# An attention and two feed-forward layers in one program: the causal mask's triangle made on GpSimd, the padding queries put in front

## The chip, the cores and the metric

One core of one Trainium2 chip runs the whole program. The metric is device time in microseconds; the runs shown of the kernel before took 1008.39, 1011.96 and 1009.94 us, median 1009.94. Five engines work side by side: TensorE (PE, with its weight loads as PEld), VectorE (DVE), ScalarE (ACT), GpSimd (POOL) and SyncE (SP, which issues all DMAs here). Each runs its own instructions in the order in which the program was written.

## The reference

Causal attention for 4 batches of 8 heads (576 positions, 64 columns a head), then two feed-forward layers over the 2304 tokens:

```python
scores = scale * q @ k.T                        # per head, 576 x 576
bias = -(cum[:, None] - cum[None, :])           # cum = cumsum(max(s, 0))
scores = where(causal, -1e9, scores + minimum(bias, 0))
attn = exp(scores - scores.max(-1))             # then / (sum + 1e-9)
x = attn @ v                                    # heads side by side: 2304 x 512
h = x @ w_in;  x = (h * cos(h)) @ w_out         # 512 -> 2048 -> 512
h = x @ w_in2; out = (max(h, 0) + log1p(exp(-abs(h)))) @ w_out2
```

## The kernel before

The program is in two parts. The attention takes the heads one after another (`emit_attention(u, ...)`, u from 0 to 31; keys and queries come in pairs of heads). The feed-forward layers follow, each in blocks of 512 or 256 tokens, with every float32 factor split into two parts and three matmuls for each product.

A head goes through these steps:

- **Maxima.** A softmax needs the largest score of each query. Six matmuls (list `MT`, L441, issued in L496 to L500) take 128 queries as weights (`taq`, 66 rows: 64 columns of the head and two for cum) against the keys they may see (`tak`). The list holds (query block, first key, width, column of the result, place in the bank). DVE reads the PSUM bank, adds `mask` and reduces to one number a query (L504). The queries are padded from 576 to 640 with the padding behind, so query block i sees keys up to 128(i+1) - 1: widths 128, 256, 384, 512 and 320 + 256, in all 1856 columns a head.
- **Maxima to rows.** DVE joins the last block's two results (L510), a matmul with `eye` transposes them, ACT copies them out (L516), and a POOL select spreads them over rows 96 to 128 of `taq` (L518, 32 x 640 elements), where rows of -1 in `tak` subtract them in the next product.
- **Scores.** Seven stretches of keys by queries in five banks (list `STL`, L442), keys on the partitions: a product with the low parts (`tbk`, `tbq`), then for the five stretches that hold a diagonal block a matmul of `tri` through `ident` (128 columns, 64 for the last), which adds -1e30 above the diagonal, then the main product (`tak`, `taq`, 128 rows). ACT takes the exponential of each bank into one of four buffers `pf` (L558).
- **Values.** `pf` times the values with a column of ones, float32 (two passes a matmul), summed in banks 5 to 7 (L570, `final` closes a sum); ACT copies the sums out (L532) and SP sends them to memory.

Rows 64 to 96 of `tak` and `taq` hold the two cum rows and otherwise zeros. There are three sets ("slots") of these buffers in the memory that the later weights (`wlate`) take over after the attention; POOL fills their constant parts at the start (L353 to L372), and `mask`, `ident`, `tri` and `eye` with selects (a select, `affine_select`, keeps an element or writes a fill value, by an affine test on its place).

The order of the instructions is made by a planner (`Planner.plan`, L95): every operation has a due time and a list of what it reads and writes; the planner steps through a modelled time with a cost for each operation (an engine and nanoseconds, such as 1000.0 for L518's select) and writes for each engine, among what is ready, the one due first, on PE with a term for weight loads. While PE has nothing ready at the start it writes filler matmuls (L376, `warm`, 256 columns each, to bank 7). So a changed cost or a changed list moves instructions on every engine, though their due times stay; what happens on the chip then is that each engine follows its own list and waits where something is not there yet. A part of the first layer's weights is converted on DVE and ACT during the attention (L421 to L438).

Of the kernel before, what the change touches and what calls it, by code (L numbers as in the profile page):

```python
# [8 lines left out]
F32 = mybir.dt.float32  # L9
# [13 lines left out]
QS = (0, 256, 576)  # L23
EARLY, SLOT = 8, 4992
# [10 lines left out]
BIG = -3.0e38  # L35
ONE_LO = 1.0 - 2.0 ** -24
# [181 lines left out]
def act_t(n, psum=False):  # L218
    return n * 0.8333 + (52 if psum else 93)
# [6 lines left out]
def build(tc, qk, v, s, w1, w2, out):  # L226
# [8 lines left out]
    def T(name, shape, dt=F32):  # L235
        return sb.tile(shape, dt, name=name, tag=name)
# [32 lines left out]
    ident = T("ident", [128, 128], BF16)  # L269
    tri = T("tri", [128, 128], BF16)  # L270
# [7 lines left out]
    lnb = T("lnb", [128, 1])  # L278
    sraw, cum = heads[0][0:32], heads[2][0:32]
# [55 lines left out]
    V.memset(zero, 0.0)  # L335
    V.memset(mask, 0.0)
    V.memset(ident, 1.0)
    V.memset(tri, 0.0)
# [9 lines left out]
    for i in (2, 0, 1):  # L348
# [4 lines left out]
        fill(vt, tak.bitcast(F32)[64:96, :, 0:S], 0.0, ag)  # L353
# [3 lines left out]
        fill(vt + 2, taq.bitcast(F32)[0:96, :, S:], 0.0, [(("cq", i), 0)])  # L357
        fill(vt + 3, taq.bitcast(F32)[64:96, :, 0:S], 0.0, [(("augq", i, h), "z") for h in range(2)])
        P.op(vt + 4, [(POOL, 700.0, lambda taq=taq: G.memset(taq.bitcast(F32)[64:66, :, 0:S], 1.0))], r=[(("augq", i, h), "z") for h in range(2)], w=[(("augq", i, h), 0) for h in range(2)])
        if i == 2:  # L360
            P.op(vt + 8, [(POOL, 660.0, lambda: G.affine_select(out=mask, in_=mask, pattern=[[-1, 640]], compare_op=ALU.is_ge, fill=BIG, base=512, channel_multiplier=1))],
                 (), [("mask", 0)])
            P.op(vt + 9, [(POOL, 250.0, lambda: G.affine_select(out=ident, in_=ident, pattern=[[-1, 128]], compare_op=ALU.is_equal, fill=0.0, base=0, channel_multiplier=1))],
                 (), [("ident", 0)])
            P.op(vt + 10, [(POOL, 250.0, lambda: G.affine_select(out=tri, in_=tri, pattern=[[1, 128]], compare_op=ALU.is_ge, fill=-1.0e30, base=0, channel_multiplier=-1))],  # L365
                 (), [("tri", 0)])
# [74 lines left out]
    MT = [[(4, 0, 320, 4, 0), (0, 0, 128, 0, 320)], [(1, 0, 256, 1, 0), (4, 320, 256, 9, 256)], [(2, 0, 384, 2, 0)], [(3, 0, 512, 3, 0)]]  # L441
# [9 lines left out]
    def emit_attention(u, at, st):  # L451
# [9 lines left out]
        if sl == 0:  # L461
# [3 lines left out]
            if u == 0:  # L465
                t = at(-8)
                for x in range(2):
                    dma(t + x, raw[:, x], qk[0, :, x], w=[kr[x]])
                    P.op(t + 2 * x + 4, [(ACT, act_t(S), lambda x=x: A.activation(tak[0:64, x, 0:S], raw[0:64, x], AF.Copy))], r=[kr[x]], w=[kk[x]])
                    P.op(t + 2 * x + 5, [(ACT, act_t(S), lambda x=x: A.activation(taq[0:64, x, 0:S], raw[64:128, x], AF.Copy, scale=0.125))], r=[kr[x]], w=[kq[x]])  # L470
# [64 lines left out]
        for x, lst in enumerate(STL):  # L535
# [4 lines left out]
            for i, (j, qs, off, w) in enumerate(lst):  # L540
# [3 lines left out]
                if x != 1:  # L544
                    ml.append((o[:, 0:min(w, 128)], ident, tri[:, :min(w, 128)], False, False, True, 0))
# [244 lines left out]
```

## Time and profile before

| | us |
|---|---|
| runs shown, median | 1009.94 |
| profiled execution | 1008.23 |
| its span | 1006.4 |
| PE busy | 998.8 (99%) |
| DVE busy | 690.5 |
| ACT busy | 604.0 |
| POOL busy | 51.2 |

The span runs from the first to the last instruction of the profiled execution; 1.8 us lie around it. A busy time is the union of an engine's instructions; matmuls overlap in the records, so that a matmul's own duration is longer than the step from one start to the next. TensorE's granted clock is 1.00, the full 2.4 GHz, in every window asked for. The attention runs until about 211 us, the feed-forward layers from there to the end.

### The profile page before, as it was taken

How to read it: one execution, taken by the hardware profiler on the slowest of the kernel's cores; microseconds unless marked ns; L12 is line 12 of the kernel's file. 1: busy time of each engine (PE TensorE's matmuls, PEld its weight loads, DVE VectorE, ACT ScalarE, POOL GpSimd, SP SyncE). 2: the span in 40 equal slices, each digit the busy share in tenths (PEclk: the TensorE clock that was granted, in tenths of full speed). 3: DMA queues.
4: the chain of work that ended last, by engine and by line, in shares of the span. 5: the costliest groups of instructions: out<-in, count | busy, mean ns of one | idle time of the engine just before them, and what ended most of it. 6: DMA issues, size and time to landing. Idle time of an engine off the chain costs nothing.

```text
span 1006.4 us, 14198 instructions
## 1 busy us (share of the span) xinstructions
PE 998.8 (99%) x5180; PEld 842.3 (84%) x5180; DVE 690.5 (69%) x1284; ACT 604.0 (60%) x1062; POOL 51.2 (5%) x68
## 2 busy tenths in 40 slices
PE   9999999999999999999999999999999999999998
PEld 7888888878888889988888888888888998888886
DVE  8889888879964536445357989995565756555553
ACT  5777777777655445555456668665454655445444
POOL 8111112100000000000000000000000000000000
PEclk9999999999999999999999999999999999999999
DMA  6676666663422212002012335221130201001001
GB/s 209 212 209 188 194 189 185 190 211 113 155 84 91 90 51 101 26 22 64 1 65 99 135 130 189 88 80 49 35 115 1 84 1 42 1 1 42 1 1 42
DMA packets 40488, 95.29 MB, mean 95 GB/s; under 512 B 7074, under 2 KB 13730, under 8 KB 36322
## 3 DMA queue, kind: packets, MB, share of 16 engines
q1 hardware_dynamic: 40418, 94.39, 29.5%
q8 instruction: 40, 0.66, 0.3%
q14 instruction: 30, 0.25, 0.1%
HBM read 66.87 MB, written 18.64 MB: 85 GB/s over the span
## 4 chain that ended last, share of the span: by engine, by line
PE 93%; DVE 2%; DMA 2%; POOL 1%; issue 1%; ACT 0%; SPq 0%; DVEq 0%; POOLq 0%; ACTq 0%
PE bank L322 93%; PE bank L376 1%; DMA stage<-w 1%; DVE bc L504 1%; DMA adram<-num 0%; POOL wlate L330 0%; DMA raw<-rdram 0%; DMA raw<-adram 0%; DVE wlate L488 0%; DVE wlate L486 0%; DVE conv L429 0%; DMA rd<-adram 0%; DVE xl L308 0%; DVE raw L614 0%; POOL tri L365 0%
## 5 line engine op out<-in xcount | busy, mean ns | idle before, releaser
L322 PE MATMUL bank<-xh,wearly 128*128 128x512 f32 (+1 forms) x640 | 193.8, 369 | 1.2 <-DVE pf L658 1.2
L322 PE MATMUL bank<-xh,wlate 128*128 128x512 f32 (+1 forms) x640 | 193.7, 368 | 0.0
L322 PE MATMUL bank<-ghi,wlate 128*128 128x512 f32 (+1 forms) x640 | 193.5, 368 | 0.0
L322 PE MATMUL bank<-ghi,wearly 128*128 128x512 f32 (+1 forms) x640 | 193.5, 368 | 0.0
L299 ACT ACTIVATE ghi<-pf 128x512 fp32r<-128x512 f32 (+1 forms) x160 | 93.8, 587 | 141.9 <-DVE pf L670 92.0
L308 DVE TENSOR_TENSOR glo<-pf,ghi 128x512 fp32r<-128x512 f32 (+1 forms) x160 | 102.0, 637 | 77.4 <-ACT ghi L299 76.9
L322 PE MATMUL bank<-wlate 128*128 128x320 f32 (+9 forms) x576 | 150.5, 363 | 1.3 <-POOL xl L330 1.2
L322 PEld LDWEIGHTS bank<-xh,wearly 128*128 128x128 f32 x640 | 117.3, 189 | 21.7 <-DVE pf L658 1.6
L322 PEld LDWEIGHTS bank<-ghi,wlate 128*128 128x128 f32 x640 | 117.3, 189 | 20.0
L322 PEld LDWEIGHTS bank<-xh,wlate 128*128 128x128 f32 x640 | 117.3, 189 | 19.9
L322 PEld LDWEIGHTS bank<-ghi,wearly 128*128 128x128 f32 x640 | 117.3, 189 | 19.8
L322 PE MATMUL bank<-pf,vf 128*65 128x320 f32 (+4 forms) x448 | 127.9, 384 | 0.0
L322 PE MATMUL bank<-xl,wearly 128*128 128x512 f32 (+1 forms) x320 | 117.9, 369 | 0.0
L322 PE MATMUL bank<-glo,wlate 128*128 128x512 f32 (+1 forms) x320 | 117.9, 368 | 0.0
L322 PE MATMUL bank<-xl,wlate 128*128 128x512 f32 (+1 forms) x320 | 117.8, 368 | 0.0
L322 PE MATMUL bank<-glo,wearly 128*128 128x512 f32 (+1 forms) x320 | 117.8, 368 | 0.0
L322 PEld LDWEIGHTS bank<-wlate 128*128 128x128 f32 (+1 forms) x576 | 95.5, 191 | 17.7 <-POOL xl L330 1.4
L666 DVE SCALAR_TENSOR_TENSOR bc<-pf 128x512 f32<-128x512 f32 (+1 forms) x80 | 51.0, 637 | 81.7 <-ACT pf L664 81.7
L504 DVE CUSTOM_DVE_ANT_0 bc<-bank,mask 128x384 bf16<-128x384 f32 (+3 forms) x192 | 82.0, 468 | 15.7 <-PE bank L322 10.8
L558 ACT ACTIVATE pf<-bank 128x256 f32<-128x256 f32 (+2 forms) x160 | 66.7, 433 | 38.1 <-PE bank L322 33.3
L654 DVE SCALAR_TENSOR_TENSOR pf<-pf,pf 128x512 f32<-128x512 f32 (+1 forms) x80 | 50.7, 635 | 56.3 <-ACT pf L652 56.3
L663 ACT ACTIVATE pf<-bank 128x512 f32<-128x512 f32 (+1 forms) x80 | 44.3, 554 | 68.4 <-PE bank L322 65.7
(75 smaller groups left out, 1331.5 us busy)
## 6 DMA issues: line engine op xcount, KB each, us to landing
stage<-w SPq DMA_DIRECT2D x32, 1024.0 KB
raw<-qk SPq DMA_DIRECT2D x15, 576.0 KB
wlate<-wlate SPq DMA_DIRECT2D x30, 288.0 KB
vf<-v SPq DMA_DIRECT2D x32, 160.0 KB
adram<-num SPq DMA_DIRECT2D x32, 146.2 KB
xdram<-num SPq DMA_DIRECT2D x18, 256.0 KB
out<-num SPq DMA_DIRECT2D x18, 256.0 KB
raw<-adram SPq DMA_DIRECT2D x32, 128.0 KB
```

The source lines that it names most:

```text
L299: opts.append((ACT, act_t(n, psum), (lambda: A.activation(o, i, AF.Copy, scale=1.0 if scale is None else scale))))
L308: return [(DVE, dve_t(n), lambda: V.tensor_tensor(o, a, hi.bitcast(F32), op=ALU.subtract))]
L322: X.matmul(o, a, b, start=st, stop=sp, skip_group_check=skip)
L376: X.matmul(bank[7][:, 0:256], zero[:, 0:128], zero, start=True, stop=True)
L504: P.op(tx + 1, [(DVE, dve_t(w, True) + DX, lambda bk=bk, off=off, w=w, mo=mo, col=col, pr=pr, jk=junk[i if x < 2 else x - 2]: V.tensor_ten ...
L558: P.op(tx + 3, [(ACT, act_t(wt, True) + AX, lambda pt=pt, bk=bk, wt=wt: A.activation(pt[:, :wt], bank[bk][:, :wt], AF.Exp))], r=[(("bank", ...
L654: P.op(te + 2, [(DVE, dve_t(n), lambda a0=a0, a1=a1: V.scalar_tensor_tensor(a1, a1, MAGIC, a0, op0=ALU.subtract, op1=ALU.subtract))], r=[( ...
L663: P.op(te, [(ACT, act_t(n, True), lambda a0=a0, hp=hp: A.activation(a0, hp, AF.Abs))], r=hr, w=[(k0, (tg, "a"))])
L666: P.op(te + 2, [(DVE, dve_t(n), lambda a0=a0, a2=a2: V.scalar_tensor_tensor(a2, a0, 2.0, a0, op0=ALU.subtract, op1=ALU.mult, reverse0=True))],
```

## The change

Three things are changed together.

The triangle: `tri`, `ident` and their five matmuls a head go. In their place POOL writes zeros above the diagonal into the exponentials, in place in `pf`, one select for each of the five diagonal blocks (128 x 128, the last 128 x 64), after ACT's exponential and before the product with the values. So that no exponential overflows before it is cleared, rows 66 to 96 of `tak` and `taq` now hold steps of 20 positions: their product is -1.27e30 or below where a key lies in a later step than its query. Two POOL selects a slot write these steps, in place of a memset of zeros in `tak`, one in `taq` and one of ones in its two cum rows.

The padding: the 64 padding queries stand in front (`QP` = 64), so query block i sees keys up to 128 i + 63: widths 64, 192, 320, 448 and 320 + 256, in all 1600. `MT` is written anew for it, again six matmuls in four banks. All blocks now reduce 128 rows.

The order: new selects stand in the planner with 220 + 1.4 ns an element; the due times are unchanged, and the planner makes new lists for all engines.

```diff
 QS = (0, 256, 576)
+QP = 640 - S
...
+STEP, FAR = 20, -1.2676506002282294e30
...
-    ident = T("ident", [128, 128], BF16)
-    tri = T("tri", [128, 128], BF16)
...
+    cst = T("cst", [128, 2])
...
+    V.memset(cst[:, 0:1], 1.0)
+    V.memset(cst[:, 1:2], 0.0)
+    V.memset(cst[64:66, 1:2], 1.0)
     V.memset(mask, 0.0)
-    V.memset(ident, 1.0)
-    V.memset(tri, 0.0)
...
-        fill(vt, tak.bitcast(F32)[64:96, :, 0:S], 0.0, ag)
+        P.op(vt, [(POOL, 1400.0, lambda tak=tak: G.affine_select(out=tak[64:96, :, 0:S], in_=cst[64:96, 0:1].unsqueeze(2).broadcast_to((32, 2, S)), pattern=[[0, 2], [1, S]],
+                                                                 compare_op=ALU.is_ge, fill=0.0, base=STEP, channel_multiplier=-STEP))], (), ag)
         fill(vt + 1, tak.bitcast(F32)[:, :, S:], 0.0, ck)
         fill(vt + 1.5, tak.bitcast(F32)[96:128, :, 0:S], -1.0, [(("cm", i), 0)])
         fill(vt + 2, tbk.bitcast(F32)[:, :, S:], 0.0, [(("cb", i), 0)])
-        fill(vt + 2, taq.bitcast(F32)[0:96, :, S:], 0.0, [(("cq", i), 0)])
-        fill(vt + 3, taq.bitcast(F32)[64:96, :, 0:S], 0.0, [(("augq", i, h), "z") for h in range(2)])
-        P.op(vt + 4, [(POOL, 700.0, lambda taq=taq: G.memset(taq.bitcast(F32)[64:66, :, 0:S], 1.0))], r=[(("augq", i, h), "z") for h in range(2)], w=[(("augq", i, h), 0) for h in range(2)])
+        fill(vt + 2, taq.bitcast(F32)[0:96, :, 0:QP], 0.0, [(("cq", i), 0)])
+        P.op(vt + 3, [(POOL, 1400.0, lambda taq=taq: G.affine_select(out=taq[64:96, :, QP:], in_=cst[64:96, 1:2].unsqueeze(2).broadcast_to((32, 2, S)), pattern=[[0, 2], [1, S]],
+                                                                     compare_op=ALU.is_ge, fill=FAR, base=STEP, channel_multiplier=-STEP))], (), [(("augq", i, h), 0) for h in range(2)])
         if i == 2:
             P.op(vt + 8, [(POOL, 660.0, lambda: G.affine_select(out=mask, in_=mask, pattern=[[-1, 640]], compare_op=ALU.is_ge, fill=BIG, base=512, channel_multiplier=1))],
                  (), [("mask", 0)])
-            P.op(vt + 9, [(POOL, 250.0, lambda: G.affine_select(out=ident, in_=ident, pattern=[[-1, 128]], compare_op=ALU.is_equal, fill=0.0, base=0, channel_multiplier=1))],
-                 (), [("ident", 0)])
-            P.op(vt + 10, [(POOL, 250.0, lambda: G.affine_select(out=tri, in_=tri, pattern=[[1, 128]], compare_op=ALU.is_ge, fill=-1.0e30, base=0, channel_multiplier=-1))],
-                 (), [("tri", 0)])
             for x in range(3):
...
-    MT = [[(4, 0, 320, 4, 0), (0, 0, 128, 0, 320)], [(1, 0, 256, 1, 0), (4, 320, 256, 9, 256)], [(2, 0, 384, 2, 0)], [(3, 0, 512, 3, 0)]]
+    MT = [[(4, 0, 320, 4, 0), (1, 0, 192, 1, 320)], [(3, 0, 448, 3, 0), (0, 0, 64, 0, 448)], [(2, 0, 320, 2, 0)], [(4, 320, 256, 9, 0)]]
...
-                    P.op(t + 2 * x + 5, [(ACT, act_t(S), lambda x=x: A.activation(taq[0:64, x, 0:S], raw[64:128, x], AF.Copy, scale=0.125))], r=[kr[x]], w=[kq[x]])
+                    P.op(t + 2 * x + 5, [(ACT, act_t(S), lambda x=x: A.activation(taq[0:64, x, QP:], raw[64:128, x], AF.Copy, scale=0.125))], r=[kr[x]], w=[kq[x]])
...
-                dma(t + 17, taq.bitcast(F32)[0:64, :, 0:S], tbq.bitcast(F32)[64:128], r=[(ktbq, pt_)], w=kq + ([("go", 0)] if u == 2 else []))
+                dma(t + 17, taq.bitcast(F32)[0:64, :, QP:], tbq.bitcast(F32)[64:128], r=[(ktbq, pt_)], w=kq + ([("go", 0)] if u == 2 else []))
...
-                mo = 512 - 128 * qi + k0
-                pr = min(128, S - qi * 128)
+                mo = 512 + QP - 128 * qi + k0
+                pr = 128
...
-            rr = [(y, pt_) for y in (ktbk, ktbq, ktbkl, ktbql, (ktak, sl), (ktaq, sl), (kaugk, sl))] + [(kaugq, 0), (("c", rg), 0), (("cm", rg), 0), (("cb", rg), 0), ("ident", 0), ("tri", 0)]
+            rr = [(y, pt_) for y in (ktbk, ktbq, ktbkl, ktbql, (ktak, sl), (ktaq, sl), (kaugk, sl))] + [(kaugq, 0), (("c", rg), 0), (("cm", rg), 0), (("cb", rg), 0)]
                 o = bank[bk][:, off:off + w]
                 ml = [(o, tbk[:, sl, ks], tbq[:, sl, qs:qs + w], i == 0, False, True, w)]
-                if x != 1:
-                    ml.append((o[:, 0:min(w, 128)], ident, tri[:, :min(w, 128)], False, False, True, 0))
-                ml.append((o, tak[:, sl, ks], taq[:, sl, qs:qs + w], False, True, True, w))
+                ml.append((o, tak[:, sl, ks], taq[:, sl, QP + qs:QP + qs + w], False, True, True, w))
...
             pt = pf[pi]
             P.op(tx + 3, [(ACT, act_t(wt, True) + AX, lambda pt=pt, bk=bk, wt=wt: A.activation(pt[:, :wt], bank[bk][:, :wt], AF.Exp))],
                  r=[(("bank", bk), bt)], w=[(("pf", pi), bt)], table="exp")
+            done = bt
+            for i, (j, qs, off, w) in enumerate(lst):
+                if qs == 128 * j:
+                    dw = min(w, 128)
+                    P.op(tx + 4 + i, [(POOL, 220.0 + 1.4 * dw, lambda z=pt[:, off:off + dw], dw=dw: G.affine_select(
+                        out=z, in_=z, pattern=[[1, dw]], compare_op=ALU.is_ge, fill=0.0, base=0, channel_multiplier=-1))],
+                        r=[(("pf", pi), done)], w=[(("pf", pi), (bt, i))])
+                    done = (bt, i)
...
-                    P.op(at(st["av"] + x * SD) + y, mms(ml), r=[(("vo", u % 3), 0), (("vf", u % 3), tg), (("pf", pi), bt)] + old, w=[(key, (tg, "av", got[e]))])
+                    P.op(at(st["av"] + x * SD) + y, mms(ml), r=[(("vo", u % 3), 0), (("vf", u % 3), tg), (("pf", pi), done)] + old, w=[(key, (tg, "av", got[e]))])
```

PE in the middle of the attention, before: from behind a head's second product with 448 score columns and one of 320 to the first product of the 448 exponentials with the values (`pf0_94`). `bank5` to `bank7` take the value products.

```order
L322 LDWEIGHTS ident_103
L322 MATMUL bank3_68<-tri_104,ident_103 128x128
L322 MATMUL bank7_72<-pf3_97,vf_98 65x320
L322 MATMUL bank3_68<-wlate_80 128x320
L322 MATMUL bank4_69<-wlate_80 128x192
L322 LDWEIGHTS ident_103
L322 MATMUL bank4_69<-tri_104,ident_103 128x128
L322 MATMUL bank4_69<-wlate_80 128x192
L322 MATMUL bank4_69<-wlate_80 128x64
L322 LDWEIGHTS ident_103
L322 MATMUL bank4_69<-tri_104,ident_103 128x64
L322 MATMUL bank6_71<-pf0_94,vf_98 65x128
```

PE at the like place now, from the two products of 448 columns on (in `bank1`; the exponentials are in `pf1_95`):

```order
L323 MATMUL bank1_66<-wlate_80 128x448 x2
L323 MATMUL bank0_65<-wlate_80 128x256
L323 MATMUL bank7_72<-pf2_96,vf_98 65x64
L323 MATMUL bank6_71<-pf0_94,vf_98 65x320
L323 MATMUL bank3_68<-wlate_80 128x320 x2
L323 MATMUL bank5_70<-pf3_97,vf_98 65x256
L323 MATMUL bank4_69<-wlate_80 128x192 x2
L323 MATMUL bank4_69<-wlate_80 128x64
L323 MATMUL bank5_70<-pf1_95,vf_98 65x128
```

Before, three matmuls of the mask and one value product of an older exponential stand in the place (and ahead of it one more score product of 320 columns, after the second of 448); now the two products of 448 columns follow each other without a mask matmul, and three value products of older exponentials (64, 320 and 256 columns) stand between.

POOL before, from the first slot's last memsets to the constants for the mask:

```order
L330 MEMSET wlate_80 32x2x576
L330 MEMSET wlate_80 128x2x64
L330 MEMSET wlate_80 32x2x576
L330 MEMSET wlate_80 128x2x64
L330 MEMSET wlate_80 96x2x64
L330 MEMSET wlate_80 32x2x576
L359 MEMSET wlate_80 2x2x576
L361 ISA
L361 AFFINE_SELECT mask_102<-mask_102 128x640
L363 AFFINE_SELECT ident_103<-ident_103 128x128
L365 AFFINE_SELECT tri_104<-tri_104 128x128
L330 MEMSET xl1_84 128x128 x3
```

POOL now, the first slot's part:

```order
L355 AFFINE_SELECT wlate_80<-cst_105 32x2x576
L331 MEMSET wlate_80 128x2x64
L331 MEMSET wlate_80 32x2x576
L331 MEMSET wlate_80 128x2x64
L331 MEMSET wlate_80 96x2x64
L361 AFFINE_SELECT wlate_80<-cst_105 32x2x576
L364 AFFINE_SELECT mask_102<-mask_102 128x640
L331 MEMSET xl1_84 128x128 x3
```

The first slot's steps are the first thing on POOL and the last of the slot, with one long memset between them instead of three; the selects for ident and tri are gone.

POOL in the middle of the attention, now; before, only the L518 rows stood there, one a head:

```order
L517 AFFINE_SELECT wlate_80<-xh1_82 32x640
L561 AFFINE_SELECT pf0_94<-pf0_94 128x128
L561 AFFINE_SELECT pf2_96<-pf2_96 128x128
L561 AFFINE_SELECT pf3_97<-pf3_97 128x128
L561 AFFINE_SELECT pf1_95<-pf1_95 128x128
L561 AFFINE_SELECT pf0_94<-pf0_94 128x128
L517 AFFINE_SELECT wlate_80<-xl1_84 32x640
L561 AFFINE_SELECT pf0_94<-pf0_94 128x64
L561 AFFINE_SELECT pf3_97<-pf3_97 128x128
L561 AFFINE_SELECT pf0_94<-pf0_94 128x128
L517 AFFINE_SELECT wlate_80<-xh1_82 32x640
```

Five selects of the mask stand between two of the maxima's (L517), in one queue; a maxima's select can stand ahead of the 64-column mask select of an older head.

## Rows read from the trace of the kernel before

**Rows 1.** The page, busy share and instructions of each engine, and the chain by engine:

```profile
PE 998.8 (99%) x5180; PEld 842.3 (84%) x5180; DVE 690.5 (69%) x1284; ACT 604.0 (60%) x1062; POOL 51.2 (5%) x68
...
PE 93%; DVE 2%; DMA 2%; POOL 1%; issue 1%; ACT 0%; SPq 0%; DVEq 0%; POOLq 0%; ACTq 0%
```

**Rows 2.** Windows: length, busy us (x instructions), clock, DMA share, GB/s:

```profile
50.00:200.00 150.00, 149.81 (x941) 124.30 (x940) 133.20 (x393) 110.69 (x234) 24.79 (x25) 1.00 0.67 193
400.00:412.00 12.00, 12.00 (x102) 12.00 (x101) 6.91 (x16) 6.74 (x19) 0.00 (x0) 1.00 0.31 89
450.00:550.00 100.00, 100.00 (x443) 82.86 (x442) 56.28 (x79) 54.52 (x87) 0.00 (x0) 1.00 0.15 51
```

**Rows 3.** Waits, 50 to 200 us: engine, line, releaser, total us, times, longest:

```profile
PEld bank L322 <- DVE mx L504: 1.2, 4, 0.5
```

**Rows 4.** Groups by shape, 50 to 200 us: count, busy us, mean ns, idle before:

```profile
L322 PE MATMUL bank<-tri,ident 128*128 128x128 bf16 x99 | 22.6, 230 | 0.0
...
L504 DVE CUSTOM_DVE_ANT_0 bc<-bank,mask 128x512 bf16<-128x512 f32 x25 | 17.0, 681 | 0.3
...
L558 ACT ACTIVATE pf<-bank 128x448 f32<-128x448 f32 x25 | 13.5, 539 | 5.6 <-PE bank L322 5.4
L518 POOL TENSOR_SCALAR_AFFINE_SELECT wlate<-xl 32x640 fp32r<-32x640 f32 x13 | 13.2, 1017 | 75.7 <-ACT xl L516 75.7
...
L504 DVE CUSTOM_DVE_ANT_0 bc<-bank,mask 128x128 bf16<-128x128 f32 x25 | 6.9, 277 | 0.0
```

**Rows 5.** Timeline of PE, from 101 us: start, length, instruction, count:

```profile
101.46 0.23 PE L322 MATMUL bank<-tri,ident 128*128 128x128 bf16 x1
101.52 0.87 PE L322 MATMUL bank<-pf,vf 128*65 128x64 f32 x4
102.04 0.70 PE L322 MATMUL bank<-wlate 128*128 128x448 f32 x2
...
103.99 0.21 PE L322 MATMUL bank<-tri,ident 128*128 128x64 bf16 x1
104.03 0.28 PE L322 MATMUL bank<-wlate 128*128 128x64 f32 x1
...
104.69 0.23 PE L322 MATMUL bank<-tri,ident 128*128 128x128 bf16 x1
104.75 0.75 PE L322 MATMUL bank<-pf,vf 128*65 128x320 f32 x2
105.09 1.23 PE L322 MATMUL bank<-wlate 128*128 128x256 f32 x6
106.17 0.70 PE L322 MATMUL bank<-pf,vf 128*65 128x320 f32 x2
106.47 0.64 PE L322 MATMUL bank<-wlate 66*128 66x512 f32 x1
```

**Rows 6.** Timeline of all engines at the start:

```profile
0.80 4.14 POOL L330 MEMSET wlate<- 32x1152 f32 x6 [0.29 <-POOLq L783]
...
5.00 1.05 POOL L359 MEMSET wlate<- 2x1152 f32 x1
...
6.12 0.81 POOL L361 TENSOR_SCALAR_AFFINE_SELECT mask<-mask 128x640 bf16<-128x640 bf16 x1
...
7.57 1.35 DVE L486 TENSOR_TENSOR wlate<-raw,wlate 64x1152 fp32r<-64x1152 f32 x1
...
7.66 1.42 POOL L365 TENSOR_SCALAR_AFFINE_SELECT tri<-tri 128x128 bf16<-128x128 bf16 x1
...
9.51 1.15 PE L322 MATMUL bank<-wlate 66*128 66x320 f32 x6 [1.16 <-POOL xl L330]
```

**Rows 7.** Timeline of POOL and DVE, 21 to 24 us:

```profile
21.15 0.75 POOL L518 TENSOR_SCALAR_AFFINE_SELECT wlate<-xl 32x640 fp32r<-32x640 f32 x1
...
21.46 1.64 DVE L486 TENSOR_TENSOR wlate<-raw,wlate 64x1152 fp32r<-64x1152 f32 x1
...
21.85 1.86 POOL L518 TENSOR_SCALAR_AFFINE_SELECT wlate<-xh 32x640 fp32r<-32x640 f32 x1
```


## The prediction

> **What bounds the kernel now.** I read the page's busy shares and chain first [rows 1]: the reader is to see PE busy in 99% of the span and in 93% of the chain that ended last. A busy PE need not be a full PE, so the windows come next [rows 2]. In the feed-forward layers 443 matmuls of 512 columns fill 100 us, 0.226 us each, and 102 of 256 columns fill 12 us, 0.118 us each: 0.42 ns a column, and that stretch is at PE's rate. In the attention, 50 to 200 us, PE is busy 149.8 of 150 us, DVE 133.2, ACT 110.7, POOL 24.8. The group of 512-column maxima, one a head, counts 25 there [rows 4], so a head takes 6.0 us; DVE works 5.33 us of it, POOL 0.99. The waits of that stretch hold PE's longest wait for another engine: 1.2 us in total, for DVE [rows 3]. So in the attention too PE sets the time, DVE is 11% behind it, and nothing behind the attention changes: what PE is relieved of per head arrives at the end, as long as no other engine becomes later than PE.
>
> **Removed: the mask matmuls.** Each head loses four matmuls of 128 columns (tri through ident) and one of 64. Their recorded 230 ns [rows 4] is pipelined length, not price. The price is bounded by starts [rows 5]. Below: the next matmul starts 0.06 us after it (101.46 to 101.52, 104.69 to 104.75), 0.04 after the 64-column one (103.99 to 104.03): 4 x 0.065 + 0.04 = 0.30 us a head. Above: its columns are too few to cover the next matmul's weight load. The pair of 320-column products with the values behind a mask matmul spans 0.34 us from its own start to the next row's start (104.75 to 105.09), the pair without one 0.30 (106.17 to 106.47); 0.04 more each makes 4 x 0.105 + 0.07 = 0.49. I take 0.09 each and 0.04: 0.40 a head, 12.8 us over 32 heads (bounds 9.6 and 15.7).
>
> **Removed: 256 columns of maxima.** Before 512, 384, 256, 256, 320 and 128 columns, now 448, 320, 320, 256, 192 and 64. By the rate alone 256 x 0.42 ns = 0.107 us a head. A 64-column stream does not cover a weight load; if nothing under 0.1 us counts (the ident load and a mask matmul lie about there), 0.07. I take 0.07: 2.3 us in all (bounds 2.3 and 3.4). On DVE, 512 columns take 681 ns and 128 take 277 [rows 4], 1.05 ns a column, so DVE loses 0.27 us a head.
>
> **Added: the selects on POOL.** Five a head (four of 128 columns, one of 64), in place on the exponentials, between ACT's exp and the product with the values; and the maxima's own select shares the queue. No row shows a 128-column float select undisturbed. Two that were held up tell it: the 640-column one that began at 21.85 ended 0.61 us after DVE's two-input L486 (21.46 + 1.64 = 23.10), the 128-column tri one, 7.66 + 1.42 = 9.08, ended 0.16 us after L486's 8.92 [rows 6, 7]. An undisturbed 640-column one takes 0.75 (21.15), so 0.13 lies ahead of the part that is held; 128 columns make 0.13 + 0.16 = 0.3 us free. The bounds are 0.2 and the tri row's 1.42. Over the attention the 640-column select (the half of them that read xl) means 1017 ns [rows 4], 0.27 over its free time, so I take 0.3 + 0.27 = 0.57 us: POOL then works 0.99 + 5 x 0.57 = 3.8 us of a head. It is not the bound.
>
> So POOL and DVE keep each other out, and 21.85 shows it with its number. The Trainium skill ("Advanced Engine Details and Errata", section on VectorE Performance Modes) says that DVE's second SBUF port is shared with GpSimd and that the two block each other; by that rule, the trace agrees, and it speaks against moving work to POOL.
>
> What does it delay? The order shows what PE does between a head's 448-column scores and their first product with the values. Before: matmuls of 320, 128 (mask), 2 x 320 (one value product), 320, 192, 128, 192, 64, 64 columns, by the rates some 1.3 us (a value column costs 0.52 us / 640 = 0.81 ns and pass, 101.52 to 102.04 [rows 5]). That covered the exp of 0.54 us [rows 4] and its two hand-overs, which are thus 0.76 at most. Now it holds matmuls of 256, 320, 320, 192, 192 and 64 and value products of 64, 320 and 256 columns: about 1.85 us. It has to cover 0.54 + 0.3 + three hand-overs (0.76 to 1.14): 0.1 to 0.5 us spare here, near the least in the run. Held up by the mean 0.27 most selects pass; one that starts beside the 1.35 us of an L486 [rows 6] may not. Bounds of new PE waits: 0 (all covered) and 160 selects x 0.07 = 11 us (if each had 0.4 spare and the held time spread as 0 to 0.8). I take 2.5 us, near the low end, since PE waited 1.2 us in 150 for all its suppliers before [rows 3].
>
> **DVE** goes to 5.33 - 0.27 = 5.06 us, plus what the selects hold it up: between 0 and 5 x 0.16 = 0.8. L486 took 1.64 beside a 640-column select [rows 7] and 1.35 alone [rows 6], 0.29 more; a quarter as many columns, one hit in two: 0.15. So 5.2 us beside PE's 6.0 - 0.47 = 5.5: no bound, but 94% full.
>
> **The start.** Per slot POOL sets two float selects of 1152 columns in place of two memsets that took 1.05 us each [rows 6], and the ident and tri selects go. At 640 columns 0.75 a free select of 1152 is about 1.2 us, a held one up to twice that. PE's stream there is full of filler matmuls (124 before, 123 now), whose number is fixed in the order. I take 0, between -1 and +2 us.
>
> **The sum** against the profiled execution, 1008.2 us (span 1006.4, 1.8 around it): -12.8 - 2.3 + 2.5 = -12.6, so 995.6. The median of the runs shown lies 1.7 above that execution; with it 997.3. I say 997.
>
> **Rivals.** (1) PE stays the bound, as above: 994 to 1001 with the bounds of the mask price and of the waits. (2) The shared port makes DVE the pace. At the upper 0.8 a head DVE needs 5.06 + 0.8 = 5.86 us, 0.33 over PE: 0.33 x 32 = 10.6 of the 15.1 us are lost, 1005. For it: DVE's 94%. Against: a select holds the port 0.16 us, and DVE is not always after it. (3) Slower: POOL becomes the pace. If a select takes the tri row's 1.42 us, a head needs 0.99 + 5 x 1.42 = 8.1 us of POOL, 2.1 over today's 6.0: +67 us, 1077. It decides from a mean select of (6.0 - 0.99)/5 = 1.0 us. Against: the 1.42 were nearly all spent beside one DVE instruction. (4) The first select now stands at the queue's head. If it has to fetch code, the first maxima wait. Before, the mask select began 0.07 us after the memset ahead of it (5.00 + 1.05, 6.12), so no row shows such a fetch; at most the 5.3 us from 0.80 to 6.12 could have hidden one. Then the first select would run from 6.1 to 7.3, the memsets of the slot (1.05 and three short ones, about 1.0 of the six that took 4.14) to 9.4, the queries' select to 10.6, and the first maxima, which began at 9.51 [rows 6], 1.1 later: 998.4. The Trainium skill ("GPSIMD Engine Reference", Instruction dispatch) gives about 6 us for the first call of a freshly loaded kernel; by that page it would be 999, and the 0.07 us at 6.12 speak against it here.
>
> **Chances.** (1) 0.70, (2) 0.18, (3) 0.06, (4) 0.06. About 3 us (0.3%) can be told from no change. Faster: 0.70 + 0.06 + 0.13 of (2) = 0.89; same 0.04 (the rest of (2), nearly); slower 0.07. The range, 991 to 1004, has the lower end where mask price and columns come near their upper bounds with no waits (1009.9 - 19.1 = 990.8), the upper where (2) takes most; it leaves out (3), the upper part of (2) and little below.
>
> **What would show it.** Right: a head in the attention at 5.5 to 5.6 us, PE's feed-forward matmuls some 13 us earlier than before, selects of 0.3 us with a tail to 1.5, POOL at 3 to 4 us a head, DVE's mean for L486 up by 0.1 to 0.2. Wrong: PE's waits for POOL of more than 5 us in total, DVE's busy share at 98%, or a select mean above 1.0 us.

## The result: 8.5 us faster, where 13 were predicted

| | median us | runs | profiled execution |
|---|---|---|---|
| before | 1010.45 | 1008.39 to 1011.96 (4) | 1008.23 |
| changed | 1001.97 | 1001.69 to 1002.24 (4) | 1001.94, span 1000.2 |

The ratio is 0.9917 with an interval of 0.9899 to 0.9936. The direction and the range (991 to 1004) held; the value of 997 missed by 5.0 us, and the likeliest case's own range, 994 to 1001, just missed. The gain is about two thirds of the one worked out.

The page of the changed kernel, busy shares and chain (it answers to [rows 1]):

```profile
PE 987.5 (99%) x5019; PEld 839.3 (84%) x5019; DVE 683.3 (68%) x1286; ACT 604.4 (60%) x1061; POOL 124.1 (12%) x223
...
PE 91%; DMA 3%; DVE 2%; ACT 2%; POOL 1%; issue 1%; SPq 0%; DVEq 0%; ACTq 0%
```

POOL went from 5% to 12%, and PE gave up 11.3 us of busy time, while the span fell by 6.2 only. The windows say where PE now stands idle (length, busy us and instructions of PE, PEld, DVE, ACT, POOL; clock, DMA share, GB/s; the first row answers to [rows 2]):

```profile
50.00:200.00 150.00, 147.37 (x859) 128.19 (x859) 131.31 (x401) 117.52 (x249) 85.83 (x159) 1.00 0.69 196
...
450.00:550.00 100.00, 100.00 (x442) 82.81 (x442) 60.06 (x85) 56.64 (x89) 0.00 (x0) 1.00 0.20 66
```

In the attention PE is idle 2.63 us of 150, where it was 0.19. The feed-forward layers run as before. PE's waits for others, 25 to 200 us, weight loads and matmuls (total us, times, longest; they answer to [rows 3]):

```profile
PEld bank L323 <- POOL pf L561: 5.0, 14, 0.6
PEld bank L323 <- DVE mx L503: 1.3, 5, 0.4
PEld bank L323 <- ACT pf L555: 1.2, 4, 0.4
PEld bank L323 <- DMA wlate<-wlate: 1.0, 1, 1.0
...
PE bank L323 <- POOL pf L561: 2.2, 7, 0.5
```

The selects are the new first row. Over the whole span it stands at 5.6 us in 16 waits, the two more behind 200 us:

```profile
PEld bank L323 <- POOL pf L561: 5.6, 16, 0.6
```

Before, from 25 to 200 us, the weight loads' waits for other engines are these (10.5 us stand beside them in which loads of `ident` waited for no engine that the profile shows):

```profile
PEld bank L322 <- DVE mx L504: 1.2, 4, 0.5
...
PEld bank L322 <- ACT pf L558: 0.2, 1, 0.2
```

(The weight load before a matmul waits first, the matmul only for what it lets through: the rows of PEld and PE tell of the same waits and are not added.) The groups by shape, 50 to 200 us (count, busy us, mean ns, idle before; they answer to [rows 4]):

```profile
L561 POOL TENSOR_SCALAR_AFFINE_SELECT pf<-pf 128x128 f32<-128x128 f32 x106 | 53.3, 509 | 55.1 <-ACT pf L555 54.2
L517 POOL TENSOR_SCALAR_AFFINE_SELECT wlate<-xl 32x640 fp32r<-32x640 f32 x13 | 13.7, 1054 | 2.5 <-ACT xl L515 1.8
...
L485 DVE TENSOR_TENSOR wlate<-raw,wlate 64x1152 fp32r<-64x1152 f32 x11 | 15.2, 1386 | 0.3
L503 DVE CUSTOM_DVE_ANT_0 bc<-bank,mask 128x448 bf16<-128x448 f32 x25 | 15.5, 621 | 1.6 <-PE bank L323 0.6 <-ACT pf L555 0.4 <-ACT wlate L475 0.2
L555 ACT ACTIVATE pf<-bank 128x448 f32<-128x448 f32 x26 | 14.1, 541 | 6.3 <-PE bank L323 5.7 <-POOL wlate L517 0.5
```

and before:

```profile
L486 DVE TENSOR_TENSOR wlate<-raw,wlate 64x1152 fp32r<-64x1152 f32 x11 | 15.0, 1364 | 0.3
```

A select of 128 columns means 0.51 us; DVE's L485 (L486 before) is nearly as long as it was, 1386 against 1364 ns. One wait of PE for a select, in the timeline of all engines (start, length, instruction, in brackets the idle time before it and what ended it):

```profile
41.76 1.22 DVE L309 TENSOR_TENSOR wearly<-conv,wearly 128x1024 fp32r<-128x1024 f32 x1
41.82 1.31 POOL L561 TENSOR_SCALAR_AFFINE_SELECT pf<-pf 128x128 f32<-128x128 f32 x1 [0.95 <-ACT pf L555]
...
43.18 0.49 PE L323 MATMUL bank<-pf,vf 128*65 128x128 f32 x2 [0.50 <-POOL pf L561]
```

The select starts 0.06 us after a DVE instruction with two inputs and ends at 43.13, 0.15 behind DVE's end: 1.31 us for work that takes 0.29 where no such instruction runs. PE's product with the values stands 0.50 us for it. Of the 153 selects from 25 to 200 us, 111 take under 0.35 us and 30 over 0.7, up to 1.45. Of the 14 that PE's weight loads waited for, 12 ran beside a DVE instruction of 1.2 to 1.35 us and took 0.69 to 1.40 us; the other two took 0.24 and 0.29 and had stood in POOL's queue behind a maxima's select.

Three stretches make up the whole. Read from the starts in PE's timeline:

| | before | changed | |
|---|---|---|---|
| first product with the values | 23.95 | 25.49 | +1.54 |
| from there to the first feed-forward matmul | 187.12 | 178.75 | -8.37 |
| from there to the last matmul's start | 791.15 | 791.79 | +0.64 |

The sum, -6.2, is the profiled executions' difference, -6.3. The first row's place, at the start (it answers to [rows 6]):

```profile
1.22 1.15 POOL L355 TENSOR_SCALAR_AFFINE_SELECT wlate<-cst 32x1152 fp32r<-32x1152 f32 x1 [0.71 <-DVE cst L338]
2.42 1.91 POOL L331 MEMSET wlate<- 128x128 f32 x4
4.41 1.97 POOL L361 TENSOR_SCALAR_AFFINE_SELECT wlate<-cst 32x1152 fp32r<-32x1152 f32 x1
...
9.84 1.08 PE L323 MATMUL bank<-wlate 66*128 66x320 f32 x6 [2.03 <-DMA wlate<-wlate]
```

The first maxima come 0.33 us later, after 2.03 us in which PE had nothing (1.16 before). The last row's place, at the seam to the feed-forward layers, in the chain of waits (start, length, what) and in DVE's timeline:

```profile
203.79 7.45 DMA raw<-adram
211.24 0.94 issue
212.18 0.69 DVE raw L619
```

```profile
212.18 0.69 DVE L619 TENSOR_TENSOR raw<-raw,raw 128x512 f32<-128x512 f32 x1 [0.97 <-DMA raw<-adram]
...
217.06 0.69 DVE L663 TENSOR_TENSOR pf<-bank,pf 128x512 f32<-128x512 f32 x1
```

DVE stands at a transfer of the second block of tokens; the first activation's product (L663) is queued behind it, and PE waits 1.7 us for that at 216.1 (1.2 before, at 223.3, where DVE had stood 1.45 us at a transfer as well). PE now, then PE and DVE before:

```profile
217.80 0.50 PE L323 MATMUL bank<-xh,wearly 128*128 128x512 f32 x1 [1.67 <-DVE pf L663]
```

```profile
224.52 0.50 PE L322 MATMUL bank<-xh,wearly 128*128 128x512 f32 x1 [1.19 <-DVE pf L658]
...
217.70 0.69 DVE L614 TENSOR_TENSOR raw<-raw,raw 128x512 f32<-128x512 f32 x1 [1.45 <-DMA raw<-rdram]
```

### The profile page after: what moved, and what is told of

The parts are those of the page before. It is cut to its first block, busy times and chain, and to the rows that moved or that the text cites. A ratio compares the mean times of both kernels' runs of the same rounds, so it can differ in the third digit from the quotient of the medians.

```text
span 1000.2 us, 14054 instructions
## 1 busy us (share of the span) xinstructions
PE 987.5 (99%) x5019; PEld 839.3 (84%) x5019; DVE 683.3 (68%) x1286; ACT 604.4 (60%) x1061; POOL 124.1 (12%) x223
## 4 chain that ended last, share of the span: by engine, by line
PE 91%; DMA 3%; DVE 2%; ACT 2%; POOL 1%; issue 1%; SPq 0%; DVEq 0%; ACTq 0%
PE bank L323 90%; DMA wlate<-wlate 1%; DMA raw<-adram 1%; POOL pf L561 1%; ACT pf L555 1%; PE bank L375 1%; DMA adram<-num 0%; ACT wlate L476 0%; SPq L285 0%; DVE raw L619 0%; DVE bc L503 0%; DVE conv L428 0%; DVE wlate L309 0%; DMA num<-s 0%; DVE xl L309 0%
## 5 line engine op out<-in xcount | busy, mean ns | idle before, releaser
L323 PE MATMUL bank<-wlate 128*128 128x320 f32 (+9 forms) x576 | 131.9, 344 | 3.1 <-DMA wlate<-wlate 2.5
L323 PE MATMUL bank<-pf,vf 128*65 128x320 f32 (+4 forms) x448 | 121.5, 385 | 3.0 <-POOL pf L561 2.4
L503 DVE CUSTOM_DVE_ANT_0 bc<-bank,mask 128x320 bf16<-128x320 f32 (+3 forms) x192 | 74.3, 430 | 15.4 <-PE bank L323 13.5
```

The costliest lines, as they stand in the source:

```text
L323: X.matmul(o, a, b, start=st, stop=sp, skip_group_check=skip)
L503: P.op(tx + 1, [(DVE, dve_t(w, True) + DX, lambda bk=bk, off=off, w=w, mo=mo, col=col, pr=pr, jk=junk[i if x < 2 else x - 2]: V.tensor_ten ...
```

## The experiments

Three theories stood at first, a fourth came with the seam. A: the masks and columns gave what was predicted, and the selects' latency took more back than the 2.5 us allowed. B: the port shared by POOL and DVE makes DVE the pace. C: the mask matmuls were worth less, as the weight loads that they left uncovered stay. S: the seam's wait is DVE standing at the transfers of the second block of tokens, with the activations queued behind. All runs are told in one table; "attention" and "feed-forward" are the second and third stretch above, from one profile each.

| kernel | median us | ratio to before (interval) | attention | feed-forward |
|---|---|---|---|---|
| changed | 1001.97 | 0.9917 (0.9899 to 0.9936) | 178.75 | 791.79 |
| no_select | 1000.05 | 0.9885 (0.9853 to 0.9917) | 176.92 | 794.43 |
| select_aside | 999.18 | 0.9867 (0.9836 to 0.9898) | 174.01 | 793.39 |
| cost500 | 1001.50 | 0.9908 (0.9872 to 0.9944) | 176.43 | 792.13 |
| more_filler | 1003.91 | 0.9926 (0.9897 to 0.9956) | 180.33 | 792.00 |
| tri_out | 1005.81 | 0.9958 (0.9945 to 0.9972) | 183.44 | 792.86 |
| pad_only | 1008.03 | 0.9980 (0.9970 to 0.9990) | 185.82 | 791.06 |
| mask_only | 1005.16 | 0.9950 (0.9932 to 0.9968) | 181.97 | 791.90 |
| more_filler_cost500 | 1001.83 | 0.9923 (0.9902 to 0.9945) | 177.63 | 792.49 |
| seam_first | 1003.44 | 0.9938 (0.9921 to 0.9955) | 178.45 | 792.81 |
| seam_aside | 998.81 | 0.9889 (0.9873 to 0.9905) | 173.75 | 794.14 |
| seam_cost500 | 1003.66 | 0.9938 (0.9920 to 0.9956) | 176.41 | 798.28 |
| x_later | 999.29 | 0.9878 (0.9859 to 0.9898) | 179.00 | 789.33 |

The changed kernel, seam_first and x_later have one order in the attention and show 178.45 to 179.00: that is how far profiles of one order lie apart here in this stretch; their first products with the values lie further apart, 24.59 to 25.49 (see The start). The kernels ran at five different times, each time beside runs of the kernel before, so the ratios compare better than the medians. In the kernels with cost500 in their name the last product with the values stands 3.8 to 4.2 us behind the first feed-forward matmul, in the changed kernel 2.0, so some 2 us of their attention count in the last column.

**The selects taken out of the way.** no_select does not issue them; select_aside lets them run on the same data at the same places and write to a tile that nothing reads:

```diff
# no_select
-  lambda z=..., dw=dw: G.affine_select(out=z, in_=z, pattern=[[1, dw]], ...)
+  lambda z=..., dw=dw: None
# select_aside
-  out=z, in_=z, pattern=[[1, dw]]
+  out=aside[:, :min(dw, 112)], in_=z[:, :min(dw, 112)], pattern=[[1, min(dw, 112)]]
```

> The changed kernel with the order of PE, DVE and ACT kept as it is, but without POOL's five mask selects a head (the triangle of the diagonal blocks is left uncleared; nothing else is left out). Theory A (my present one: the removed matmuls gave nearly the 15 us of the forecast, and PE now waits some 6 us more than before, for the selects, by their latency): about 995 to 997 us, PE's waits for POOL gone, a head at 5.4 to 5.5 us. Theory B (the selects cost through the port that POOL and DVE share, DVE slower): the same 995 to 997. Theory C (the removed matmuls gave less, because the weight loads that lay beside them are now uncovered): 1000 to 1002, no change.

> The same order again; the selects run, read the exponentials as before, but write their result to a tile of its own that nobody reads (112 of 128 columns; the triangle is left uncleared). So no product with the values waits for them, while POOL still holds the port as long. Theory A (latency): 996 to 998 us, nearly all of what no_select gives. Theory B (port): 1000 to 1002 as the changed kernel, with DVE's two-input instructions as long as there. Theory C: 1000 to 1002.

select_aside, 25 to 200 us, weight loads' waits and (50 to 200) the selects:

```profile
PEld bank L324 <- ACT pf L556: 2.1, 7, 0.4
PEld bank L324 <- DVE mx L504: 2.0, 7, 0.5
PEld bank L324 <- DMA wlate<-wlate: 1.7, 1, 1.7
...
L562 POOL TENSOR_SCALAR_AFFINE_SELECT aside<-pf 128x112 f32<-128x112 f32 x110 | 56.0, 509 | 51.7 <-ACT pf L556 46.1 <-ACT xh L516 1.8
```

The selects take the same 509 ns and hold the port as often, yet with nobody waiting for them the attention is 4.7 us shorter (5.0 in seam_aside). That is the size of the 5.0 us of waits for POOL, and it refutes B as the pace: DVE has the same company from POOL and is not the bound. Without any select (no_select) L485 means 1376 ns, against 1386 with them. It also bears against C: the attention is 13.1 us shorter than before with other waits still in it, more than the 9.6 + 2.3 that C allows. That margin is small, but PE is also idle for 2.0 us of this stretch (171.99 us busy of 174.01), where it was for 0.2 before (186.93 of 187.12), so that its busy time fell by 14.9 us. The planner's new order is in this too; no run has it by itself.

The times show less. no_select's 1000.05 lies in C's range and outside that of A and B, and its profiled execution, the slowest of its four runs, is 1.2 us longer than the changed kernel's; select_aside's 999.18 lies between A's range and that of the others. no_select is not better than select_aside (176.92): there PE waits 4.7 us for DVE's maxima, 1.5 of it in one event:

```profile
PEld bank L323 <- DVE mx L503: 4.7, 8, 1.5
```

Both return 1.6 to 2.6 us behind the attention: the end moved up by 1.9 and 2.8 us by the medians.

**More room for the selects.** cost500 tells the planner 500 ns + 1.4 a column for a select instead of 220, so it puts the products with the values later:

```diff
-  P.op(tx + 4 + i, [(POOL, 220.0 + 1.4 * dw, ...
+  P.op(tx + 4 + i, [(POOL, 500.0 + 1.4 * dw, ...
```

> The changed kernel complete, with the planner told 500 + 1.4 ns an element for a select in place of 220 + 1.4, so that the order puts the products with the values later: about 0.2 us more lies between a 448-column score and its first product. Theory A: PE's waits for POOL fall from 7 to 3 us or less, 997 to 999.5 us. Theory B and C: within 1 us of 1002.

```profile
PEld bank L323 <- DVE mx L503: 3.7, 7, 1.2
PEld bank L323 <- ACT pf L555: 2.8, 10, 0.5
...
PEld bank L323 <- POOL pf L561: 1.3, 3, 0.7
```

The waits for POOL fall from 5.0 to 1.3, and those for DVE and ACT rise from 2.5 to 6.5. The attention's column is 2.3 us less, but about 1.8 of this stands behind the first feed-forward matmul, and the median, 1001.50, misses A's 997 to 999.5 and is not to be told from the changed kernel's. The waits moved to other engines.

**The start.** more_filler repeats the last filler matmul 18 times before the first maxima, so that PE has no gap there; more_filler_cost500 joins this with cost500:

```diff
+  order[last + 1:last + 1] = [order[last]] * 18
```

> The changed kernel with 18 more filler matmuls right before the first maxima, where PE stood idle for 2.0 us and its granted clock then fell to half from 11.6 to 15.1 us. If that half clock is what starts the values 1.5 us later than before (25.5 us against 23.9), the clock stays at 1.00, the first product with the values comes by 24.5 and the time falls by about 1 us to 1001. If the start is set by something else (the order's fillers, POOL's first selects), the clock stays up and the time does not move, 1002.

> Candidate: the selects' cost in the planner raised by 280 ns, so that they are given more room, and 18 more filler matmuls at the start. Each alone gave 1001.5 and 1003.9. Theory A: the waits for POOL fall to about 1.5 us as with the raised cost alone, first feed-forward matmul near 201, time 999 to 1001. Theory B: no better than the changed kernel, 1002.

The gap goes and the first product with the values is 0.95 us earlier (24.54), but the first feed-forward matmul is not (204.87 against 204.24), and the times are 1003.9 and 1001.8. So in these runs filling the gap brought the end no earlier. Of the 1.54 us at the first product, 0.64 are the four score matmuls of 256 columns that now stand ahead of it (24.85 to 25.49). The rest is not fixed by the order: seam_first (below) has the same order here, but in its profile the 43 filler matmuls at the start lasted longer (7.26 us against 6.63), the gap was 1.39 us, and the clock stayed at 1.00:

```profile
11.50:15.00 3.50, 3.50 (x34) 3.08 (x32) 3.50 (x20) 0.63 (x2) 3.13 (x8) 1.00 0.87 253
```

Its first product came at 24.59, 0.64 behind the kernel before, and its first feed-forward matmul at 203.04, 1.2 ahead of the changed kernel's. So about 0.9 of the 1.54 us go with the half clock of the one execution that was profiled. (seam_aside, at full clock too, has 25.13, with one more gap of 1.0 us at 18.0.) In the four runs of the changed kernel this is not seen in the time: 1001.69 and 1002.24 us at a mean granted clock of 1.00, 1001.94 and 1002.00 at 0.998.

**One part at a time.** tri_out is the kernel before in its own order with the mask matmuls not issued; pad_only has the padding and the columns alone, mask_only the selects alone:

```diff
# tri_out (in the function that issues matmuls)
+                if a is None:
+                    continue
-  ml.append((o[:, 0:min(w, 128)], ident, tri[:, :min(w, 128)], ...))
+  ml.append((o[:, 0:min(w, 128)], None, mask[:, :min(w, 128)], ...))
# pad_only: the diff without its selects, tri and ident kept
# mask_only
-QP = 640 - S
+QP = 0
-  MT = [[(4, 0, 320, 4, 0), (1, 0, 192, 1, 320)], ... (4, 320, 256, 9, 0)]]
+  MT = [[(4, 0, 320, 4, 0), (0, 0, 128, 0, 320)], ... (3, 0, 512, 3, 0)]]
```

> The kernel before, its order kept, with the mask matmuls (tri through ident) not issued and the two step rows set by selects at the start; the triangle of the diagonal blocks is not masked at all, and the columns stay 1856 a head. It prices the mask matmuls by themselves. Theory A (the price was right, 0.40 us a head, and the loss lies in waits for the selects): 12.8 us off the attention, first feed-forward matmul 11 to 13 us earlier than in the kernel before (211.1), time 997 to 999, up to 2 us more where the seam before the first gelu takes some back. Theory C (the mask matmuls were over-priced, since the uncovered weight load stays behind when they go): 9.6 us off at most, first feed-forward matmul not before 202, time above 1000.5. Theory B (the shared port) says nothing else here than A, since POOL gets no new work.

> The kernel before with the padding queries in front and 1600 columns of maxima, mask matmuls kept. The columns alone: 2.3 us less PE work by the prediction (bounds 2.3 and 3.4), first feed-forward matmul 2 to 3.5 us earlier than 211.1, time about 1007.5, hardly to be told from the kernel before; no selects on POOL, so no waits for POOL. Theory B would add that DVE's 0.27 us a head were also worth something: then over 5 us less. Theory C: the columns are worth less than 2 us as well.

> The changed kernel with the padding queries behind as before: 1856 columns of maxima, selects on POOL. Theory A: the gain of the whole change without the columns' 2.3, 1003 to 1005, PE's waits for POOL as in the changed kernel, 5 to 8 us in total, or fewer, since the longer maxima matmuls give the selects more cover. Theory B: DVE has 5.33 us and the selects' holds a head, so its waits (PE for DVE mx) rise to 5 us and more, time 1006 and above.

tri_out has 160 matmuls less, and its attention is only 3.7 us shorter. That is far from A's 12.8 and within C's bounds (9.6 at most, above 1000.5 us), but not for C's reason alone. Its waits, 25 to 200 us:

```profile
PEld bank L324 <- DVE xl L513: 5.4, 11, 1.4
PEld bank L324 <- DVE mx L507: 5.2, 13, 0.7
```

The row in [rows 3] has 1.2 us for the maxima. PE without its mask matmuls runs into DVE, which still has 1856 columns a head in an order made for a slower PE. PE is idle for 4.8 us of the stretch (178.62 busy of 183.44), so its busy time fell by 8.3 us; the waits of the weight loads may hide more of the price, and so the mask's price can't be read from this kernel. The columns seem to be worth more than their 2.3 us once PE is faster: by themselves (pad_only) they give 2.0 us by the medians, on top of the selects (from mask_only to the changed kernel) 3.2. (In pad_only's profile the attention is 1.3 us shorter, but its start has the half clock too, 0.52 from 11.5 to 15 us, and the first feed-forward matmul is 0.2 us earlier and not 2.) The parts alone give 2.0 + 4.9 = 6.9, the whole 8.1 to 8.5; by the intervals (1 to 3, 3 to 7, 6.5 to 10) this is an indication and no proof. In mask_only PE waits 5.5 us for POOL, as A said, and 2.8 us for maxima, 1.3 in the changed kernel; its 1005.16 us lie just above A's range.

**The seam.** seam_first moves the first activation's product, rounded copy and low part ahead of DVE's step that waits for the transfer; seam_aside and seam_cost500 do the same to select_aside and cost500. x_later is seam_first with the second block's steps and transfers due later:

```diff
# seam_first: in the finished order, behind the activation's sine
+    for o in (gelu, ghi0, glo0):
+        order.remove(o)
+    i = order.index(sin) + 1
+    order[i:i] = [gelu, ghi0]          # glo0 behind the DVE step that follows
# x_later, besides
-  emit_x(which, k, lambda kc, c0=c0: cb[max(c0 - 8, 0)] + kc * TUNE["xd"])
+  emit_x(which, k, lambda kc, c0=c0: cb[max(c0 - 5, 0)] + kc * TUNE["xd"])
```

> The changed kernel with its planned order, but at the seam the first activation of the feed-forward layers (its product, the rounded copy and the low part) is moved ahead of the scaling of the next block of tokens, for whose transfer VectorE waited 0.97 us. Theory A (the loss is latency of the selects and what the seam takes back): PE's wait at the seam, 1.7 us (PE) and 2.1 (weight loads), falls under 0.5, the end moves up by 1 to 1.5 us, 1000.5 to 1001. Theory S (the seam only passes on a lateness that comes from the transfers of the block behind it): the wait goes there and comes back some microseconds later, at a later activation or at the second block; 1002.

> The kernel whose selects write to a tile that nothing reads (so no product with the values waits for them, and the triangle is not cleared), with the seam as in seam_first. Without the seam edit it took 999.2 with 2.6 us of wait at the seam. Theory A: both losses taken away, so the time of the prediction without its 2.5 us of waits and with 1 to 1.5 us of later start: 996 to 997.5. Theory S: 999.

> Candidate: the planner's cost of a select raised by 280 ns (1001.5 alone) and the seam as in seam_first. Theory A: 1000 to 1000.5, 1.3 us less than the raised cost alone. Theory S: 1001.5.

> seam_first with the scaling of the second block of tokens due three eighths of a segment later (its transfers and VectorE steps stand behind the first and the second activation of the feed-forward layers, 25 us and more before TensorE needs them); the attention's order is that of the changed kernel up to the first feed-forward matmuls. Theory S (the seam's wait is VectorE standing at that block's transfers, with the activations queued behind): no wait over 0.5 us on TensorE from 205 to 235 us, the stretch from the first to the last feed-forward matmul back at 791.1, as in the kernel before, and 1 to 2 us less time than seam_first, 1000.5 to 1002. Theory T (the wait belongs to the activations' own chain): 2 us and more of wait stay, 792.8 as in seam_first, and 1003.

seam_first: the wait at the first activation is gone, and a longer one stands at the second (PE's waits, 205 to 235 us, and DVE's timeline):

```profile
PE bank L323 <- DVE glo L309: 2.9, 1, 2.9
...
221.33 0.69 DVE L620 TENSOR_TENSOR raw<-raw,raw 128x512 f32<-128x512 f32 x1 [1.71 <-DMA raw<-adram]
...
224.81 0.68 DVE L309 TENSOR_TENSOR glo<-pf,ghi 128x512 fp32r<-128x512 f32 x1
```

Again DVE stands at a transfer of that block, and the activation's low part is queued behind it. So theory S held against A: moving one activation only passes the lateness on. seam_aside waits 2.9 us at the second activation too. In seam_cost500 DVE stands 2.9 us at a transfer and PE waits 2.6 and 1.2 us for activations; its 798.28 us also hold a stretch of lower clock (0.57 from 232 to 236 us). By the time, seam_aside's 998.81 is what S said; seam_first's 1003.44 and seam_cost500's 1003.66 lie above what either theory said, with runs from 1001.33 to 1005.64 and from 1001.22 to 1005.51. x_later takes the transfers' steps out from between the activations:

```profile
211.56 0.69 DVE L665 TENSOR_TENSOR pf<-bank,pf 128x512 f32<-128x512 f32 x1
212.17 0.68 DVE L620 TENSOR_TENSOR raw<-raw,raw 128x512 f32<-128x512 f32 x1
212.95 0.69 DVE L309 TENSOR_TENSOR glo<-pf,ghi 128x512 fp32r<-128x512 f32 x1
```

No DVE step waits for a transfer there, PE's only wait from 200 to 240 us is 0.3 us in the attention, and the feed-forward stretch takes 789.33 us: 2.5 less than in the changed kernel and 1.8 less than before. That is more than expected (791.1, and 1000.5 to 1002 us in all); the kernel before had such a wait too, of 1.2 us. Its attention is the changed kernel's. At 999.29 us (998.50 to 1000.29, 4 runs) it beats both kernels: its ratio's interval, 0.9859 to 0.9898, ends just under where the changed kernel's begins, and its profiled execution, 999.73, is 2.2 under the changed kernel's. It has seam_first's move in it as well; no run has the later transfers alone.

## Why the prediction was right in sign and short by a third

- **Mask matmuls and columns, 15.1 us: held, as far as the runs reach.** select_aside's attention is 13.1 us shorter than before, with waits of the weight loads in it that the kernel before hardly had (2.1 us for ACT, 1.7 for a DMA), and PE's busy time there is 14.9 us less. C as it was put, 9.6 + 2.3, does not fit that. A direct price of the mask by itself failed with tri_out, so how the 15.1 divide is not shown, nor what part the planner's new order has in them.
- **New waits, 2.5 us: the step that failed, a size.** Taking the waits for the selects away gives 4.7 to 5.0. The mechanism was the one written down (0.1 to 0.5 us of spare time, a held select beside a long DVE instruction), and the bounds 0 to 11 held it. What misled was the choice of the value near the low end from PE's 1.2 us of waits: those were waits for other suppliers and say nothing of the new one. The working has a slip: by its own two rates, the columns that it lists come to 1.1 and 1.6 us and not to 1.3 and 1.85. The traces are nearer to what it took (median of 32 heads, from the end of a head's second 448-column product to its first value product: 1.35 us before, 2.03 in select_aside), so the slip is not what failed. Counted afterwards, it is 14 waits of 0.36 us in 175 us, 11 of them at a select of 0.8 us or more, where 30 of 153 selects took over 0.7. The mean select (0.51, predicted 0.57) says nothing of it; the tail does.
- **Other waits, not in the sum: about 2 us.** It is what is left over, -8.4 against -15.1 + 4.7; the rows of its size are the waits for ACT's exponentials and one transfer, 1.2 and 1.0 against 0.2 and none before. select_aside, where no product waits for a select, still has PE idle for 2.0 us against 0.2 before, which is of that size. No run took these waits away alone.
- **The start, 0: 1.5 us late**, inside its bounds of -1 to +2. Of this 0.6 is the order, and about 0.9 goes with the half clock in the profiled execution, which seam_first, with the same order there, did not have: that part is chance.
- **Behind the attention, "what PE is relieved of arrives at the end": wrong by 0.6 us**, and by 1.6 to 2.6 where the attention was shorter still. The seam is paced by transfers.
- These make 2.2 + 2.0 + 1.5 + 0.6 = 6.3, the distance from 995.6 to 1001.94. The 1.7 us added for the median did not come back: the changed kernel's median is its profiled time.
- **Rival 2, DVE the pace: no.** DVE is busy 131.3 of 150 us, 88% against the 98% named; L485 grew by 0.02 us and not 0.1 to 0.2. The two keep each other out in one direction here: selects took up to 1.45 us in place of 0.29, L485 1386 ns in place of 1364. The time that this rival would have given, 1005, was 3.0 us from the measured 1001.97, and 997 was 5.0 from it, so the time alone would have spoken for the wrong one. **Rival 3**: no, a mean select of 0.51. **Rival 4**: no, the first select runs from 1.22 to 2.37 and the memset behind it starts 0.05 later.
- **The signs.** FF matmuls 13 us earlier: 6.8 (204.24 against 211.07). A head of 5.5 to 5.6 us: 178.75 / 32 = 5.59, but by the same division it was 5.85 before, not the 6.0 that the count of 25 gave, so this sign is met from 8.0 us on of the 12.6 forecast. PE's waits for POOL of more than 5 us in total were named as a sign of being wrong: they are 5.0 from 25 to 200 us and 5.6 over the whole span, so that sign was met, and the time was short as it said.

## To carry to other kernels

When work moves from the bound engine to an idle one on the path between two others, look for its price in the tail of its durations against the spare time there, wait by wait, and not in its mean or in the idle engine's share. What the bound engine is relieved of shows only as far as its suppliers keep up, so a cut in the supplier (here 256 columns on DVE) can be worth more together with the cut in the bound engine than alone; the runs here indicate it and do not prove it. And look at the next seam: in-order queues behind a transfer gave back part of the gain there, and it paid to move the step that stood at the transfer, where moving one of those behind it did not.

## What the runs showed of the hardware beyond that

- In the changed kernel's profile, behind the 2.03 us without PE work before the first maxima, the granted clock fell to its lower level (1.2 GHz of 2.4). The same order did not always bring it: seam_first and seam_aside, with gaps of 1.39 and 1.06 us there, kept the full clock, and pad_only, with 1.80 us, fell. The windows of the changed kernel, and of more_filler, which had no gap (columns as above):

```profile
11.50:15.00 3.50, 3.50 (x19) 2.68 (x17) 3.33 (x18) 0.28 (x1) 3.13 (x8) 0.52 0.90 240
```

```profile
11.50:15.00 3.50, 3.50 (x33) 3.09 (x32) 3.50 (x22) 0.54 (x3) 3.12 (x8) 1.00 0.86 250
```

  The slow stretch ran 19 matmuls instead of 33, mostly filler, and more_filler's first feed-forward matmul was no earlier for the full clock, seam_first's was by 1.2 us. At the seam a gap of 3.65 us (no_select) was followed by full clock, one of 2.95 (seam_aside, to 221.43) by a mean of 0.59 from 222 to 226 us.
- A 128 KB transfer of token data, issued 0.46 us behind a weight transfer of 1024 KB, landed 7.45 us after its start (203.79 to 211.24).
